# Which engine's queue holds the empty instruction between the two chains of an output product

## The chip, the cores and the metric

The program runs on one core of a Trainium2 chip, as one launch. The metric is the device time of that launch in microseconds (us). Before the change three runs took 1582.14, 1582.5 and 1580.37 us; their median is 1582.14 us. One more execution was profiled; it took 1579.73 us, and its trace spans 1577.9 us. All times inside the program are counted from the start of that span.

Five engines run their own queues of instructions in order and meet only at semaphores: TensorE (PE in the rows, PEld for its weight loads), VectorE (DVE), ScalarE (ACT), GpSimd (POOL) and SyncE (SP). SyncE computes nothing here; its queue issues nearly all transfers. A q behind an engine's name in a row (SPq, ACTq) marks what its sequencer does by itself: issuing a transfer, or waiting.

## The reference

Two attentions over 2048 rows with 32 heads of 18 columns (D = 576), each with its own input and weights; the outputs stand side by side. The first (A) looks at 8 keys per row, at distances 0, 2, ... 14; the second (B) at all 2048 keys.

```python
def _A_ref(x, wqkv, wo):          # W, dil = 8, 2
    qkv = (x @ wqkv) -> q, k, v
    idx = pos[:, None] - arange(W)[None, :] * dil
    logits = einsum("bhsd,bhswd->bhsw", q, k[idx]) * scale   # masked where idx < 0
    o = einsum("bhsw,bhswd->bhsd", softmax(logits), v[idx])
    return o.reshape(B, S, D) @ wo
def _B_ref(x, wqkv, wo):
    qkv = (x @ wqkv) -> q, k, v
    p = softmax(einsum("bhqd,bhkd->bhqk", q, k) * scale)
    o = einsum("bhqk,bhkd->bhqd", p, v)
    return o.reshape(B, S, D) @ wo
return concatenate([_A_ref(A...), _B_ref(B...)], axis=-1)
```

## The kernel before

After the projections (until about 470 us) the program walks through 512 steps. A step is one group of four heads, one block of 512 queries and one tile of 128 keys: `NG` = 8 groups of 64 steps, a block every 16. In a step TensorE makes four banks of scores (line 285), ScalarE takes their exponentials (line 293), TensorE multiplies these with the values and adds up in the bank `po` (line 766). Beside that TensorE makes scores once more for a block that comes later (line 161), of which VectorE takes the maxima (line 169).

The order of each engine's queue is that in which the Python code calls its instructions; nothing rearranges it. Work with a due time is put on an agenda by step (`later`, `plan`) and called by `due` when its step comes. So the transfers that SyncE issues stand in one line, in the order of the steps, and a transfer that waits for something holds up all behind it.

Which transfers stand there in this phase:

- after a block of queries: the denominators are taken out of the result (`den<-o`, line 809), their reciprocals are written to memory (`drec<-den`, line 811) and read back spread over the rows (`rec<-drec`, line 812), some steps later the finished block is stored (`do<-n`, line 801). Line 812 waits until the write of line 811 has landed;
- the rows of a coming group's queries and keys (`qs<-dqk`, line 144, and `ks<-dqk`, line 143), 288 KB each;
- the row maxima put into a coming block (`qs<-mh` and `qs<-mt`, line 200), 2 KB each;
- for attention A, which runs on GpSimd: its inputs (`aq<-da`, `akv<-da`, line 974) and results (`dao<-...`, line 1044), and the results read back as operands of its output product (`at<-dao`, `ahl<-dao`, lines 1059 and 1061).

An output product of A is 28 small matmuls (line 1347) in two chains: one on the lower half of TensorE's rows, one on the upper half, both adding into one bank of PSUM. `together` lays such a product over two steps. It calls the first chain among the scores and maxima of the odd heads, then an empty instruction, then the second chain among those of the even heads. The empty instruction (line 1358) waits for the last matmul of the first chain (line 1359), and the first matmul of the second chain waits for the empty instruction (line 1362), so that no matmul of the second chain starts into the bank before the first chain is done. There are 32 such pairs of steps, at 610 us to 1460 us; 27 of them stand ahead of the last group. TensorE's queue goes on in order: while the first matmul of the second chain waits, no score, maximum or product behind it starts.

ScalarE's queue at that place holds the exponentials of the pair; the one that stands behind the empty instruction belongs to a score that TensorE makes ahead of the second chain.

Of the kernel before, what the change touches and what calls it, by code (L numbers as in the profile page):

```python
# [22 lines left out]
NG = H // 4  # L23
# [38 lines left out]
def two_attentions(ctx: ExitStack, tc, xa, wa, woa, xb, wb, wob, out):  # L62
# [5 lines left out]
    nc = tc.nc  # L68
# [13 lines left out]
    def bank(kind=None):  # L82
        r = rings[kind or ring]
        r.append(r.pop(0))
        return p_bank.tile([128, 512], F32, name=f"bank{r[-1]}")
# [154 lines left out]
    def maximum(r, ps=None):  # L240

        ps = ps or bank()
        (take, reduce), piece = next_piece(r)
        take(ps, *piece)
        return lambda: reduce(ps, *piece)
# [4 lines left out]
    def sync(ins, other):  # L250

        tc.add_manual_dep(ins.ins, other.ins.name,
                          mybir.DependencyInfo(mybir.DependencyClass.Sync, mybir.DependencyReason.DATA), reason="one bank")
# [24 lines left out]
    def score(g, b, kt, h, kind="scores", between=None, put_off=False):  # L278

        assert (g, b) in placed  # L280
        qs, ks = sets[g % 3]
        p, r = divmod(h, 2)
        ps = bank(kind)
        at = slice(64 * r, 64 * r + 56)
        awaiting(nc.tensor.matmul(ps, ks[at, p, 128 * kt : 128 * kt + 128], qs[at, b, p], start=True, stop=True))  # L285
        if between:
            between()

        def exponential():
            counted[0] += 1  # L290
            early = counted[0] % 12 < 6
            e = (e_room if early else work).tile([128, 512], F32, name="e", bufs=6)
            nc.scalar.activation(e, ps, AF.Exp, scale=SCALE)  # L293
            return e

        return exponential if put_off else exponential()
# [1032 lines left out]
    def together(both, y):  # L1329

        at = [(*divmod(s // NT, NB), s % NT) for s in (step, step + 1)]
        es = [[None] * 4 for _ in range(2)]
        ps = bank("scores")[:, : y.shape[1]]
        held = rings["scores"].pop()
        exps = deque()

        def one(i, h):
            f = score(*at[i], h, put_off=True)
            exps.append(lambda: es[i].__setitem__(h, f()))

        def others(r):
            return [f for i in range(2) for h in (r, r + 2)
                    for f in (lambda i=i, h=h: one(i, h), lambda: maximum(r)())[:: 1 - 2 * r]]

        def piece(r, k):
            a, b = both[r][k]
            return nc.tensor.matmul(ps, a, b, start=r == k == 0, stop=r == 1 and k == len(both[1]) - 1)  # L1347

        def in_turn(*lanes):

            for _, f in sorted(((at + every * k, f) for fs, at, every in lanes for k, f in enumerate(fs)), key=lambda p: p[0]):
                f()
                while len(exps) > 1:
                    exps.popleft()()

        last = []
        in_turn(([lambda k=k: last.append(piece(0, k)) for k in range(len(both[0]))], 0, 133), (others(1), 1, 235))
        between = nc.scalar.nop()
        sync(between, last[-1])
        upper = others(0)  # L1360
        if leaving:
            upper[2] = lambda f=upper[2], copy=leaving.pop(): (f(), exps.popleft()(), copy())
        in_turn(([lambda k=k: sync(piece(1, k), between) if k == 0 else piece(1, k) for k in range(len(both[1]))], 240, 133),
                (upper, 0, 235))
        while exps:
            exps.popleft()()
        nc.scalar.activation(y, ps, AF.Copy)
        rings["scores"].append(held)
        rings["scores"].append(rings["scores"].pop(0))
        return [(*at[i], es[i]) for i in range(2)]  # L1370
# [4 lines left out]
    while step < ALL:  # L1375
# [6 lines left out]
        if inside and inside[0] in for_two and kt and len(ready) == 1 and total - sum(given) >= 8 and step + 4 < ALL:  # L1382
            new = together(*inside.pop(0)(False))
            assert not leaving
            due()
            step += 1
            weigh(*ready, new[0])
            ready[:] = new[1:]
            due()
            step += 1  # L1390
            continue
# [77 lines left out]
```

## Time and profile before

| what | before |
|---|---|
| median of three runs | 1582.14 us |
| profiled execution, its own time | 1579.73 us |
| span of its trace | 1577.9 us |
| TensorE busy | 1569.6 us (99%), granted clock 1.0 |
| VectorE busy | 1377.1 us (87%) |
| ScalarE busy | 1207.4 us (77%) |
| GpSimd busy | 969.7 us (61%) |
| transfers issued by SyncE | 1036 |
| empty instructions on line 1358 | 32, all in ScalarE's queue |

A busy share is an average over phases with different limits, and the end of a matmul is modelled, so that 99% doesn't mean that TensorE works at its peak. Idle time of an engine that isn't the one waited for costs nothing. A row of the timeline gives the start in us, the length in us, the engine, the source line and what is written from what; a number behind an x says how many instructions are merged in it. For an instruction that only waits, and for a transfer's issue, the row begins when the wait is over: the wait is the empty time ahead of it. The length of an issue is the time on SyncE; when the data has landed shows only in who waits for it. A row of the view of stretches gives the stretch, its length, the busy time of each engine, then the granted clock, the mean busy share of the 16 transfer engines and GB/s.

### The profile page before, as it was taken

What the parts mean: (1) busy time and instruction counts of PE and PEld (TensorE: products, weight loads), DVE (VectorE), ACT (ScalarE), POOL (GpSimd) and SP (SyncE); (2) the same over time, 40 slices, a digit from 0 to 9 for tenths busy, and PEclk for the clock granted to TensorE, in tenths of its full rate; (3) what the DMA queues carried; (4) which work ended last, traced back from release to release, by engine and by line L of the source; (5) the groups of instructions that cost most, each with busy time, mean ns of one, the idle gap of its engine ahead of it and who ended that gap; (6) DMA issues with size and microseconds to landing.
All of it is one profiled execution on the core that took longest, in us unless ns stands there. A gap on an engine that the chain in (4) does not pass through costs nothing.

```text
span 1577.9 us, 34942 instructions
## 1 busy us (share of the span) xinstructions
PE 1569.6 (99%) x13272; PEld 966.4 (61%) x13272; DVE 1377.1 (87%) x2333; ACT 1207.4 (77%) x2411; POOL 969.7 (61%) x803
## 2 busy tenths in 40 slices
PE   9999999999999999999999999999999999999998
PEld 7998899999644445445445445444444444545686
DVE  5289999999999999999989999999999999998633
ACT  6424432121799999999999999999999999998654
POOL 2416742210266995995896897897798799682000
PEclk9999999999999999999999999999999999999999
DMA  9948954532312362245325325421721332154311
GB/s 242 240 147 218 270 164 131 138 107 81 62 41 65 73 142 77 64 122 108 75 77 131 89 81 117 120 79 50 149 85 50 91 95 57 51 167 131 140 57 69
DMA packets 188168, 175.65 MB, mean 111 GB/s; under 512 B 119432, under 2 KB 133512, under 8 KB 186272
## 3 DMA queue, kind: packets, MB, share of 16 engines
q1 hardware_dynamic: 182992, 161.73, 37.4%
q0 software_dynamic: 4032, 10.63, 3.3%
q8 instruction: 104, 1.70, 0.5%
q10 hardware_dynamic: 976, 1.07, 0.2%
q14 instruction: 64, 0.52, 0.1%
HBM read 98.77 MB, written 73.47 MB: 109 GB/s over the span
## 4 chain that ended last, share of the span: by engine, by line
PE 93%; DVE 3%; DMA 3%; ACT 1%; SPq 0%; issue 0%; DVEq 0%; ACTq 0%
PE po L766 30%; PE bank L285 19%; PE bank L161 17%; PE bank L380 14%; PE bank L1347 4%; PE bank L1244 3%; PE bank L571 2%; DVE mx L169 2%; PE bank L317 2%; DMA dqk<-ohi 1%; DMA dqk<-olo 1%; DMA qs<-mh 0%; PE bank L1212 0%; ACT e L293 0%; DMA raw<-xa 0%; SPq L530 0%
## 5 line engine op out<-in xcount | busy, mean ns | idle before, releaser
L169 DVE TENSOR_REDUCE mx<-bank 128x2 f32<-128x512 f32 x2048 | 1278.1, 684 | 109.1 <-PE bank L161 81.9
L293 ACT ACTIVATE e<-bank 128x512 f32<-128x512 f32 x2048 | 1047.9, 605 | 80.5 <-PE bank L285 78.0
L161 PE MATMUL bank<-ks,qs 54*128 54x512 f32 (+1 forms) x2464 | 785.8, 380 | 1.6 <-ACT y L1249 0.3
L161 PEld LDWEIGHTS bank<-ks,qs 54*128 54x128 f32 x2464 | 403.2, 184 | 387.6 <-DVE mx L169 341.1
L285 PE MATMUL bank<-qs,ks 56*128 56x512 f32 x2048 | 592.8, 426 | 0.1
L766 PE MATMUL po<-e,v 128*19 128x512 f32 x4096 | 531.7, 599 | 0.5
L285 PEld LDWEIGHTS bank<-qs,ks 56*128 56x128 f32 x2048 | 309.1, 185 | 21.3 <-ACT e L293 14.6
L987 POOL TENSOR_TENSOR pr<-aq,akv 128x1024 f32<-128x1024 f32 x72 | 158.3, 2200 | 16.7 <-PE po L766 13.8
L1029 POOL TENSOR_TENSOR pr<-lg,akv 128x1024 f32<-128x1024 f32 x72 | 158.3, 2198 | 0.6
L766 PEld LDWEIGHTS po<-e,v 128*19 128x19 f32 x4096 | 73.7, 97 | 138.2 <-issue 132.9
L991 POOL TENSOR_TENSOR pr<-pr 128x1024 f32<-128x1024 f32 x64 | 152.6, 2384 | 5.0
L715 ACT ACTIVATE ohi<-bank 128x512 f32<-128x512 f32 (+1 forms) x56 | 30.4, 594 | 149.2 <-issue 134.3
L380 PE MATMUL bank<-xhi,ahi 64*128 64x512 f32 (+1 forms) x448 | 112.9, 386 | 0.0
L380 PE MATMUL bank<-xhi,alo 64*128 64x512 f32 (+1 forms) x448 | 111.7, 387 | 0.0
L380 PE MATMUL bank<-xlo,ahi 64*128 64x512 f32 (+1 forms) x448 | 110.4, 387 | 0.0
L1347 PE MATMUL bank<-wohi,at 64*128 64x288 f32 x480 | 103.3, 305 | 0.0
L1030 POOL TENSOR_TENSOR pr<-pr 128x512 f32<-128x512 f32 x72 | 92.4, 1284 | 5.6
L430 POOL TENSOR_TENSOR alo<-raw,ahi 128x512 fp32r<-128x512 f32 (+1 forms) x14 | 17.6, 1254 | 122.6 <-ACT ahi L429 94.6
L1347 PEld LDWEIGHTS bank<-wohi,at 64*128 64x128 f32 x480 | 74.6, 184 | 27.6 <-ACT e L293 23.8
L525 POOL TENSOR_TENSOR olo<-olo,ohi 128x512 fp32r<-128x512 f32 x36 | 46.2, 1293 | 70.3 <-ACT ohi L524 60.6
L104 POOL CAST mh<-mt 128x32 fp32r<-128x32 f32 x32 | 6.7, 210 | 114.0 <-DVE mt L186 114.0
L1347 PE MATMUL bank<-wolo,at 64*128 64x288 f32 x240 | 70.3, 293 | 0.0
(210 smaller groups left out, 1864.9 us busy)
## 6 DMA issues: line engine op xcount, KB each, us to landing
do<-n SPq DMA_DIRECT2D x30, 512.0 KB
da<-ohi SPq DMA_DIRECT2D x52, 256.0 KB
akv<-da SPq DMA_DIRECT2D x64, 175.5 KB
out<-y SPq DMA_DIRECT2D x31, 288.0 KB
qs<-dqk SPq DMA_DIRECT2D x30, 288.0 KB
ks<-dqk SPq DMA_DIRECT2D x30, 288.0 KB
at<-dao SPq DMA_DIRECT2D x60, 128.0 KB
rec<-drec SPq DMA_DIRECT2D x29, 256.0 KB
```

The costliest lines, as they stand in the source:

```text
L161: return awaiting(nc.tensor.matmul(ps if part is None else ps[:, 256 * r : 256 * r + 256], qs[at, b, p, 128 * t : 128 * t + 128], ks[at, p ...
L169: nc.vector.tensor_reduce(at, ps.rearrange("q (s n) -> q s n", s=2), axis=AX.X, op=ALU.max)
L285: awaiting(nc.tensor.matmul(ps, ks[at, p, 128 * kt : 128 * kt + 128], qs[at, b, p], start=True, stop=True))
L293: nc.scalar.activation(e, ps, AF.Exp, scale=SCALE)
L380: nc.tensor.matmul(ps, a, b, start=start, stop=stop)
L766: nc.tensor.matmul(po[32 * i : 32 * i + 19], vs[g][:, kt, 19 * i : 19 * i + 19], es[i], start=kt == 0, stop=kt == NT - 1)
L987: nc.gpsimd.tensor_mul(pr, ap(st["q"][:, 2 * c], (SUB, 2), (0, W), (1, SUB)), window(st["k"], c))
L991: nc.gpsimd.tensor_add(st["pr"], st["pr"], pr)
L1029: nc.gpsimd.tensor_mul(at, ap(st["lg"], (0, 2), (SUB, W), (1, SUB)), window(st["v"], c))
L1030: nc.gpsimd.tensor_add(at[:, :, :4], at[:, :, :4], at[:, :, 4:])
L1244: nc.tensor.matmul(sums_[r], *both[r][i], start=i == 0, stop=last)
L1347: return nc.tensor.matmul(ps, a, b, start=r == k == 0, stop=r == 1 and k == len(both[1]) - 1)
```

## The change

The empty instruction goes into SyncE's queue, except where the first of the two steps is in the last group.

```diff
         last = []
         in_turn(([lambda k=k: last.append(piece(0, k)) for k in range(len(both[0]))], 0, 133), (others(1), 1, 235))
-        between = nc.scalar.nop()
+        between = (nc.scalar if at[0][0] == NG - 1 else nc.sync).nop()
         sync(between, last[-1])
```

27 of the 32 move, 5 stay. No matmul, exponential, maximum or transfer is added, removed or called in another order; the empty instruction itself has no row below, its waits show at the next row of its queue and at the matmul that waits for it.

TensorE's queue, at the first matmul of the second chain (line 1347) of the pair at 715 us; - is before, + is the change:

```order
 L285 MATMUL bank_11203<-qs_3497,ks_3498 128x512 [waits Activation_49]
 L161 MATMUL bank_11207<-ks_89,qs_88 128x512 [waits DVE_49]
-L1347 MATMUL bank_11161<-wohi,at_10878 128x288 [waits Activation_sequencer_49]
+L1347 MATMUL bank_11161<-wohi,at_10878 128x288 [waits SP_sequencer_49]
 L1347 MATMUL bank_11161<-wohi,at_10879 128x288
 L285 MATMUL bank_11212<-qs_3497,ks_3498 128x512 [waits Activation_49]
```

The matmul stands where it stood; it now waits for SyncE's sequencer. The rows behind it, scores (line 285) and the rest of the chain, are held with it.

SyncE's queue at the same pair; akv are inputs of attention A, DMAHW are the semaphores of earlier transfers:

```order
 L812 DMA rec<-drec 128x1x512 [waits DMAHW4_49,DMAHW1_49]
 L974 DMA akv<-da 32x18x78 [waits DMAHW5_49]
-L974 DMA akv<-da 32x18x78 [waits DMAHW6_49]
+L974 DMA akv<-da 32x18x78 [waits PE_49,DMAHW6_49]
 L809 DMA den<-o 128x1x16 [waits DMAHW7_49,Activation_49]
 L302 DMA v<-dv 128x1216 [waits DMAHW0_49]
```

The empty instruction stands ahead of the second `akv<-da`: behind `rec<-drec`, which waits for two transfers, and ahead of `den<-o`.

SyncE's queue at the pair at 961 us:

```order
 L812 DMA rec<-drec 128x1x512 [waits DMAHW7_49,DMAHW5_49]
 L974 DMA akv<-da 32x18x78 [waits DMAHW0_49]
-L144 DMA qs_88<-dqk 18x8x512 [waits DMAHW1_49,PE_49]
+L144 DMA qs_88<-dqk 18x8x512 [waits PE_49,DMAHW1_49]
 L200 DMA qs_1511<-mh 2x8x32 [waits DMAHW2_49,Pool_49]
 L200 DMA qs_1511<-mh 2x8x32 [waits DMAHW3_49]
```

Here the empty instruction stands ahead of a load of query rows and of the row maxima; the wait for TensorE that now comes first in the row of line 144 is that of the empty instruction.

## The prediction

> **What bounds the kernel now.** First the page's busy times and its chain of waits.
>
> ```profile
> PE 1569.6 (99%) x13272; PEld 966.4 (61%) x13272; DVE 1377.1 (87%) x2333; ACT 1207.4 (77%) x2411; POOL 969.7 (61%) x803
> PE 93%; DVE 3%; DMA 3%; ACT 1%; SPq 0%; issue 0%; DVEq 0%; ACTq 0%
> ```
>
> The chain that ends last runs on TensorE for 93% of the span and on SyncE's queue for none of it. So a microsecond in which TensorE's queue stands still lengthens the program by nearly as much, while SyncE may wait as it likes as long as nobody waits for SyncE. The change makes TensorE wait for SyncE at 27 places.
>
> Next, what one such place costs today: the view of line 1358, all of it and at the pair at 715 us, and TensorE's timeline there.
>
> ```profile
> L1358 ACTq EVENT_SEMAPHORE  x32: 17/17/17, 610.1 to 1460.4; - x32
> L1358 ACTq EVENT_SEMAPHORE  x1: 17/17/17, 715.8 to 715.8; - x1
> 715.36 0.29 PE L1347 MATMUL bank<-wolo,ahl 64*128 64x288 f32 x1
> 715.80 0.41 PE L161 MATMUL bank<-ks,qs 54*128 54x512 f32 x1
> 715.83 0.40 PE L1347 MATMUL bank<-wohi,at 64*128 64x288 f32 x1
> ```
>
> The first chain ends at 715.36 + 0.29 = 715.65, the empty instruction runs at 715.8, the second chain starts at 715.83. Both signals together take 0.18 us, and the matmul of line 161 that stands ahead of it in the queue starts only at 715.80. So the wait is hidden but for 0.03 us. The last thing to read is therefore SyncE's timeline: is SyncE past the row ahead of the empty instruction when the first chain ends?
>
> **What is removed.** If SyncE answered at once, the second chain could start with the matmul ahead of it: at most 0.03 us earlier here, some 27 x 0.03 = 0.8 us in all. How fast SyncE answers TensorE can be read where a load of operands waits for the last matmul of a product.
>
> ```profile
> 624.16 0.29 PE L1347 MATMUL bank<-wohi,ahl 64*128 64x288 f32 x1
> 624.47 0.36 SPq L1059 DMA_DIRECT2D at<-dao  x1
> 607.35 2.15 SPq L200 DMA_DIRECT2D qs<-mt  x4
> ```
>
> 624.47 - 624.45 = 0.02 us: no slower than ScalarE's sequencer. I take nothing for an open place, with -0.8 us as one end, and +0.05 us for each of the 27, or +1.4 us, as the other (a signal that took half of today's 0.18 us path more). The last row shows the tightest of the open places: the transfers ahead of the first empty instruction are issued by 607.35 + 2.15 = 609.50, and the first row of line 1358 is at 610.1. At 24 of the 27 places SyncE's timeline has the row ahead issued before the empty instruction's present time, so that it would be standing ready.
>
> The 17 ns of the empty instruction's row say nothing of this. [...] By the rows alone the change would cost 27 x 0.017 = 0.5 us.
>
> **The three places where SyncE is late.** At the pair at 715 us SyncE's timeline and its longest wait read:
>
> ```profile
> 709.89 0.35 SPq L811 DMA_DIRECT2D drec<-den  x1
> 712.20 0.59 SPq L974 DMA_DIRECT2D akv<-da  x1
> 724.18 0.60 SPq L812 DMA_DIRECT2D rec<-drec  x1
> 724.83 0.55 SPq L974 DMA_DIRECT2D akv<-da  x1
> SPq L812 <- DMA drec<-den: 8.1, 1, 8.1
> ```
>
> The empty instruction will stand behind the transfer at 724.83. That one is issued by 725.38, because `rec<-drec` ahead of it waits for the write of the reciprocals (`drec<-den`), which was issued at 709.89 and has landed only at 724.18. Nothing in this wait depends on TensorE. With 0.1 us for the signals (the rest of the 0.18 us once TensorE has long signalled) the second chain starts at 725.48 instead of 715.83: **9.6 us**. All of TensorE's queue stands behind it, so it is lost whole. The same at 854 us and at 1136 us:
>
> ```profile
> 854.74 0.40 PE L1347 MATMUL bank<-wohi,at 64*128 64x288 f32 x1
> 849.45 0.35 SPq L811 DMA_DIRECT2D drec<-den  x1
> 862.14 0.57 SPq L812 DMA_DIRECT2D rec<-drec  x1
> 862.81 0.59 SPq L809 DMA_DIRECT2D den<-o  x1
> ```
>
> Here the empty instruction stands between line 812 and line 809: free at 862.71, start at 862.81 instead of 854.74, **8.1 us**.
>
> ```profile
> 1136.14 0.40 PE L1347 MATMUL bank<-wohi,at 64*128 64x288 f32 x1
> 1126.49 0.35 SPq L811 DMA_DIRECT2D drec<-den  x1
> 1137.63 0.59 SPq L812 DMA_DIRECT2D rec<-drec  x1
> 1138.27 0.56 SPq L974 DMA_DIRECT2D akv<-da  x1
> ```
>
> Free at 1138.83, start at 1138.93 instead of 1136.14: **2.8 us**. Together 20.5 us.
>
> Why the small write takes 14.3, 12.7 and 11.1 us there shows against a calm place:
>
> ```profile
> 633.01 0.33 SPq L811 DMA_DIRECT2D drec<-den  x1
> 634.98 0.59 SPq L812 DMA_DIRECT2D rec<-drec  x1
> 1105.00:1136.00 31.00, 31.00 (x255) 14.19 (x254) 29.62 (x52) 29.90 (x60) 22.51 (x22) 1.00 0.76 158
> ```
>
> With nothing ahead of it, it is answered in 2.0 us; at the late places 288 KB loads of rows stand ahead of it in the same queue, and the transfer engines are busy for 0.76 of the stretch.
>
> [...]
>
> **What is held back.** At places where SyncE now runs ahead, the rows behind the empty instruction wait for TensorE from now on. Mostly that is a load needed much later. It matters where held rows pile up in front of a later late write. At 1103 us:
>
> ```profile
> 1103.67 0.40 PE L1347 MATMUL bank<-wohi,at 64*128 64x288 f32 x1
> 1101.08 2.40 SPq L144 DMA_DIRECT2D qs<-dqk  x3
> 1103.53 0.61 SPq L974 DMA_DIRECT2D aq<-da  x1
> 1104.18 1.55 SPq L144 DMA_DIRECT2D qs<-dqk  x2
> ```
>
> Five loads of rows move back by up to 1103.6 - 1101.1 = 2.5 us, and from 1105 to 1136 the transfer engines have no pause (the row above), so the write at 1126.49 lands later by 0 to 2.5 us; nearer to the upper end, I take 2. At 961 us:
>
> ```profile
> L1358 ACTq EVENT_SEMAPHORE  x1: 17/17/17, 960.8 to 960.8; - x1
> 955.24 0.82 SPq L144 DMA_DIRECT2D qs<-dqk  x1
> 956.16 2.29 SPq L200 DMA_DIRECT2D qs<-mh  x4
> 958.55 2.56 SPq L200 DMA_DIRECT2D qs<-mt  x4
> 963.15 4.00 SPq L144 DMA_DIRECT2D qs<-dqk  x5
> 965.00:995.00 30.00, 29.95 (x250) 14.21 (x246) 29.08 (x53) 28.65 (x57) 13.00 (x9) 1.00 0.64 148
> 994.40 0.58 SPq L812 DMA_DIRECT2D rec<-drec  x1
> 995.55 0.60 SPq L974 DMA_DIRECT2D aq<-da  x1
> 997.50 0.39 PE L1347 MATMUL bank<-wohi,at 64*128 64x288 f32 x1
> ```
>
> The load and eight small transfers, issued from 955.24 to 961.11 (5.9 us), start at 960.8 at the earliest and end at 966.7; with line 809 (0.59 us at 862.81 above, 0.7 to the next row) the loads of 963.15 begin at 967.4, 4.3 us later. The transfer engines are busy without pause to 995 (0.64). If the whole 4.3 us reach the write ahead of `rec<-drec` at 994.40, the row ahead of the next empty instruction is issued not by 996.15 but by 1000.45, and the second chain of the pair at 997.50 starts 3.0 us late. Bounds 0 and 3.0; I take 2, since part may be made up on the way. One load each is held ahead of the other two late places:
>
> ```profile
> 675.73 0.84 SPq L144 DMA_DIRECT2D qs<-dqk  x1
> ```
>
> This one would wait for the pair at 681 us, some 5.5 us; the row behind it (`den<-o`) waits for ScalarE until after that pair, as now, so nothing more is held. The load itself takes the transfer engines a part of these microseconds later on: 0 to 1 us, I take 0.5 for both places.
>
> **What is given back.** While TensorE stands, VectorE and ScalarE work off what they hold. In the row of 965 to 995 they are busy 29.08 and 28.65 of 30 us, so they hold little; 0 to 3 us over three stalls, I take 1.
>
> **Sum**, in us: 9.6 + 8.1 + 2.8 + 2 + 2 + 0.5 - 1 = 24. Against the profiled execution's own time: 1579.73 + 24 = 1603.7. The median of the runs is 2.4 us above that execution, so I forecast 1582.1 + 24 = **1606 us**.
>
> **The rivals.**
> *More places become late.* For it: held rows shift the whole queue, and open places have little room (0.6 us at 610 us). Against it: most held rows are followed by a row that waits for TensorE or ScalarE anyway. Three more stalls like the smallest, 3 x 2.8, on top of the upper bounds of the held terms (2.5 + 3 + 1): 20.5 + 6.5 + 8.4 = 35 us, 1617 us.
> *Half of the stalls vanish.* The write lands earlier once TensorE's later rows push no transfers, or other engines make good more than I allow. Against it: the loads ahead of the write are issued before the stall. 10 us, 1592 us.
> *SyncE is in time everywhere.* Only if the write were answered in the 2.0 us of the calm place. Then just the open places count: no change, 1582 us.
> *Faster.* ScalarE's queue no longer stands at the empty instruction until the first chain ends; if the exponential behind it is what TensorE waits for next, each of the 27 pairs gains up to the 0.18 us of today's path: 27 x 0.18 = 4.9 us, 1577 us. It decides only if the three late places are in time as well. Against it: the second chain starts 0.03 us behind the matmul ahead of it.
>
> **How the numbers follow.** Chances: forecast 0.66 (its own range 1600 to 1612), more late places 0.14, half of the stalls 0.12, in time everywhere 0.04, faster 0.04. About 0.2% (3 us) is what a measurement of this kernel can tell from no change. The range of 8 in 10 reaches from between the halved case and the forecast to near the case of more late places: 1596 to 1616. Slower: 0.66 + 0.14 + 0.12 = 0.92; same 0.04; faster 0.04.
>
> **What would show it.** Right: the row of line 1358 on SyncE 27 times; TensorE with a hole of about 9.6, 8 and 3 to 5 us at the pairs that are now at 715, 854 and 1136 us, each ended by SyncE right behind `rec<-drec`, and one of 1 to 3 us at the pair now at 997; the chain of waits with some 2% on line 811's write; other pairs as long as now. Wrong: no such holes, holes at many more pairs, or a second chain that starts later than now at open places.

## The result and the profile after

The changed kernel takes 1615.87 us (median of four runs, 1614.43 to 1617.46) against 1582.02 us of the kernel before on the same chip: a ratio of 1.022, 95% interval 1.0209 to 1.0232, or 33.9 us more. The forecast was 24 us more. The profiled execution took 1614.43 us, its trace spans 1612.6 us, 34.7 us more than before; the following is told by that trace.

First the page of the changed kernel: busy times, the clock in 40 slices (a digit is tenths of full speed, 9 is 90% or more), the chain of waits.

```profile
PE 1579.4 (98%) x13272; PEld 972.4 (60%) x13272; DVE 1378.3 (85%) x2333; ACT 1207.0 (75%) x2411; POOL 970.4 (60%) x803
PEclk9999999999999999999998999999999999999999
PE 79%; DMA 7%; DVE 2%; SPq 1%; ACT 0%; issue 0%; POOL 0%; DVEq 0%; ACTq 0%
```

With the same 13272 matmuls TensorE is busy 1579.4 us, 9.8 us longer than before; the mean granted clock of the run is 0.99 instead of 1.0, and one slice shows an 8. Transfers now make 7% of the chain, where they made 3%.

Line 1358, and what waits for it (in the second part: idle time in us, how often, longest):

```profile
L1358 SPq EVENT_SEMAPHORE  x27: 17/17/17, 609.7 to 1399.1; - x27
L1358 ACTq EVENT_SEMAPHORE  x5: 17/17/17, 1417.3 to 1495.2; - x5
```

```profile
PE bank L1347 <- SPq L1358: 24.4, 4, 8.2
```

27 empty instructions are SyncE's, as the diff says, and TensorE waits for SyncE at exactly four places. Its timeline there (idle time ahead of a row in brackets), and the second chain of the pair behind the first hole:

```profile
723.71 0.60 PE L1347 MATMUL bank<-wohi,at 64*128 64x288 f32 x1 [7.75 <-SPq L1358]
873.75 0.61 PE L1347 MATMUL bank<-wohi,at 64*128 64x288 f32 x1 [8.16 <-SPq L1358]
1022.03 0.40 PE L1347 MATMUL bank<-wohi,at 64*128 64x288 f32 x1 [2.71 <-SPq L1358]
1168.38 0.60 PE L1347 MATMUL bank<-wohi,at 64*128 64x288 f32 x1 [5.77 <-SPq L1358]
...
755.07 0.40 PE L1347 MATMUL bank<-wohi,at 64*128 64x288 f32 x1
```

The same row of the kernel before:

```profile
744.50 0.40 PE L1347 MATMUL bank<-wohi,at 64*128 64x288 f32 x1
```

The four are the pairs that stood at 715, 854, 997 and 1136 us. Taking each pair's start in the old trace from that in the new gives the loss step by step: the 715 pair starts 723.71 - 715.83 = 7.9 us later, but the next pair 755.07 - 744.50 = 10.6 us later. So 2.7 us are lost between the two pairs, where no empty instruction stands. It is the same behind each hole:

| pair, time before | forecast | lost at the hole, counted from the pair before | lost from there to the next pair |
|---|---|---|---|
| 715 us | 9.6 | 8.1 | 2.7 |
| 854 us | 8.1 | 8.75 | 2.8 |
| 997 us | 2 | 3.1 | 1.6 |
| 1136 us | 2.8 + 2 | 6.4 | 2.2 |
| two held loads | 0.5 | in the rows above | |
| everywhere else | -1 (given back) | -0.9 | |
| sum | 24 | 25.4 | 9.3 |

25.4 + 9.3 = 34.7 us, the difference of the spans. Where SyncE stands at the late places (its timeline):

```profile
709.32 0.35 SPq L811 DMA_DIRECT2D drec<-den  x1
722.40 0.60 SPq L812 DMA_DIRECT2D rec<-drec  x1
723.05 1.23 SPq L974 DMA_DIRECT2D akv<-da  x2
860.16 0.35 SPq L811 DMA_DIRECT2D drec<-den  x1
873.06 0.58 SPq L812 DMA_DIRECT2D rec<-drec  x1
1021.34 0.59 SPq L974 DMA_DIRECT2D aq<-da  x1
1155.11 0.35 SPq L811 DMA_DIRECT2D drec<-den  x1
1167.07 0.59 SPq L812 DMA_DIRECT2D rec<-drec  x1
1167.71 0.56 SPq L974 DMA_DIRECT2D akv<-da  x1
```

Each hole ends within 0.11 us of the row ahead of the empty instruction: 723.05 + half of 1.23 is 723.67 and the matmul starts at 723.71; 873.64 and 873.75; 1021.93 and 1022.03; 1168.27 and 1168.38. At the third, `rec<-drec` is issued at 1020.20 and two more rows stand between it and the empty instruction. At the three late places of the prediction `rec<-drec` follows its write by 13.1, 12.9 and 12.0 us (14.3, 12.7 and 11.1 before).

What is lost behind the holes shows in the view of stretches (after the five busy times: granted clock, share of the transfer engines, GB/s):

```profile
715.40:719.30 3.90, 0.56 (x4) 0.13 (x2) 1.53 (x3) 1.74 (x4) 3.82 (x2) 1.00 0.62 157
719.30:723.70 4.40, 0.00 (x0) 0.00 (x0) 0.00 (x0) 0.00 (x0) 4.24 (x3) 0.51 0.57 117
723.70:729.50 5.80, 5.79 (x31) 3.65 (x35) 2.08 (x3) 2.20 (x4) 4.30 (x3) 0.50 0.90 151
729.50:735.00 5.50, 5.50 (x48) 2.44 (x40) 4.14 (x9) 4.30 (x9) 2.00 (x3) 0.99 0.48 79
...
873.70:879.70 6.00, 5.95 (x31) 3.65 (x35) 2.94 (x7) 2.20 (x4) 0.47 (x2) 0.50 0.13 45
1023.00:1026.40 3.40, 3.40 (x24) 1.77 (x24) 1.89 (x3) 1.75 (x4) 2.05 (x3) 0.52 0.70 152
1168.40:1173.30 4.90, 4.90 (x27) 3.44 (x31) 2.08 (x3) 2.20 (x4) 2.45 (x3) 0.50 0.83 145
```

TensorE's idle time in the first hole begins at 723.71 - 7.75 = 715.96; 3.3 us later, at 719.3, the granted clock falls to a half. It is still at a half when TensorE starts again, for another 5.8 us, and then back at once. The 31 matmuls of that stretch have a spacing of 5.8 / 31 = 0.19 us, the 48 of the next 5.5 / 48 = 0.11 us. The four stretches at half clock with TensorE at work add up to 5.8 + 6.0 + 3.4 + 4.9 = 20.1 us; done at half speed, that would lose 10 us, and 9.3 us are missing. The output product itself shows the pace, two matmuls of the first chain ahead of the hole and two of the second behind it:

```profile
714.87 0.29 PE L1347 MATMUL bank<-wolo,at 64*128 64x288 f32 x1
715.01 0.29 PE L1347 MATMUL bank<-wohi,ahl 64*128 64x288 f32 x1
...
724.12 0.44 PE L1347 MATMUL bank<-wohi,at 64*128 64x288 f32 x1
724.36 0.44 PE L1347 MATMUL bank<-wolo,at 64*128 64x288 f32 x1
```

One follows the other after 0.14 us ahead of the hole and 0.24 us behind it.

So at the first hole the clock is at a half (0.50) from 719.3 to 729.5, 10.2 us, and behind the third for 3.4 us. How long TensorE has to stand for it, these four places don't tell: the third hole idles for 2.71 us only, and the clock falls all the same.

### The profile page after: what moved, and what is told of

The parts are those of the page before. It is cut to its first block, busy times and chain, and to the rows that moved or that the text cites. A ratio compares the mean times of both kernels' runs of the same rounds, so it can differ in the third digit from the quotient of the medians.

```text
span 1612.6 us, 34942 instructions
## 1 busy us (share of the span) xinstructions
PE 1579.4 (98%) x13272; PEld 972.4 (60%) x13272; DVE 1378.3 (85%) x2333; ACT 1207.0 (75%) x2411; POOL 970.4 (60%) x803
## 4 chain that ended last, share of the span: by engine, by line
PE 79%; DMA 7%; DVE 2%; SPq 1%; ACT 0%; issue 0%; POOL 0%; DVEq 0%; ACTq 0%
PE po L766 28%; PE bank L285 17%; PE bank L161 15%; PE bank L380 11%; PE bank L1347 4%; PE bank L1244 3%; DMA drec<-den 3%; DVE mx L169 2%; DMA qs<-dqk 1%; DMA do<-n 1%; DMA dqk<-olo 1%; DMA dqk<-ohi 0%; PE bank L1212 0%; DMA at<-dao 0%; PE bank L1176 0%
## 5 line engine op out<-in xcount | busy, mean ns | idle before, releaser
L1347 PE MATMUL bank<-wohi,at 64*128 64x288 f32 x480 | 107.1, 313 | 24.4 <-SPq L1358 24.4
L380 PE MATMUL bank<-xlo,ahi 64*128 64x512 f32 (+1 forms) x448 | 114.5, 387 | 0.0
```

What stands on the lines that cost most here:

```text
L380: nc.tensor.matmul(ps, a, b, start=start, stop=stop)
```

## The experiments

The diffs stand against the changed kernel and leave out the lines that count. `turn_of` in them counts the calls of `together` from 0, so that 4, 8, 14 and 18 are the four pairs with a hole. Each time stands beside the median of the kernel before on the same chip (1580.29 to 1580.56 us). The theory is: the loss is four holes and the half clock behind them, and nothing else.

**The open places alone.** The 23 other empty instructions stand on SyncE.

```diff
-        between = (nc.scalar if at[0][0] == NG - 1 else nc.sync).nop()
+        between = (nc.scalar if at[0][0] == NG - 1 or turn_of[0] in (4, 8, 14, 18) else nc.sync).nop()
```

> The empty instruction goes to SyncE at 23 of the 27 pairs; the pairs that had a hole (now at 715, 865, 1019 and 1162 us of the changed kernel) keep it on ScalarE. Theory (only the holes and TensorE's halved clock behind them cost time): no hole, granted clock 1.0 throughout, time of the kernel before, 1582 us within 2 us. Rival (each signal through SyncE, or the holding back of transfers, costs something too): 1585 us or more, with second chains that start later at the 23 pairs.

1582.28 us, ratio 1.0013 (1.0004 to 1.0022): 2 us of the 34, no wait of TensorE for SyncE, clock 1.0. So an open place costs nothing that counts. The 2 us come up behind the 17th and the 28th pair: there TensorE waits 1.1 us for VectorE's maxima (line 169) and 0.7 us for row maxima that a transfer puts into a block (`qs<-mt`, line 200), where it waited for neither before. Why these come later is not settled.

**Transfers held, without a wait of TensorE.** The kernel before, with a second empty instruction on SyncE that waits for the first chain but that nobody waits for.

```diff
-        between = (nc.scalar if at[0][0] == NG - 1 else nc.sync).nop()
+        between = nc.scalar.nop()
         sync(between, last[-1])
+        if at[0][0] < NG - 1:
+            sync(nc.sync.nop(), last[-1])
```

> The kernel before, with its empty instructions on ScalarE, and at the 27 pairs a second one in SyncE's queue that waits for the end of the first chain and that nobody waits for: SyncE's transfers are held back as in the change, TensorE waits for ScalarE alone. Theory (holding back transfers matters only by making SyncE later where TensorE waits for it): no holes, granted clock 1.0, the kernel before within 3 us. Rival (transfers that come late stop TensorE or GpSimd by themselves): 5 us or more above it.

1582.28 us, ratio 1.0007 (0.9998 to 1.0016). Holding transfers back costs 2.5 us at most, the end of the interval, as long as TensorE doesn't wait for what stands behind them.

**Three late places alone.**

```diff
-        between = (nc.scalar if at[0][0] == NG - 1 else nc.sync).nop()
+        between = (nc.sync if turn_of[0] in (4, 8, 18) else nc.scalar).nop()
```

> The empty instruction goes to SyncE at three pairs alone, those where the trace of before had SyncE late (715, 854, 1136 us); so nothing is held back ahead of them. Theory (holes as read from the trace of before, plus half of the time that TensorE runs at half clock behind each): holes of 9.6, 8.1 and 2.8 us, behind the two long ones some 2.7 us each, behind the short one 0 to 1.7 us: 20.5 + 5.4 to 7.1, so 1608 to 1610 us; the pair at 997 us has no hole. Rival (the extra time of the change came from holding back alone): 1582 + 20.5 = 1602.5 us.

1603.49 us, ratio 1.0143 (1.0126 to 1.016): 23.2 us more, between the two expectations. By its trace the holes take 9.1, 9.0 and 2.0 us, 20.1 in all, and the stretches behind them 2.1, 2.3 and 0.2 us. Both parts are there behind the two long holes. The third, without holders ahead of it, shrinks from 6.4 to 2.0 us, and behind it the clock stays full (its row of the timeline, and the stretch behind it):

```profile
1159.40 0.40 PE L1351 MATMUL bank<-wohi,at 64*128 64x288 f32 x1 [1.66 <-SPq L1362]
1159.20:1162.50 3.30, 3.10 (x31) 2.12 (x35) 1.89 (x3) 1.92 (x4) 3.14 (x4) 1.00 0.61 121
```

The 997 pair has no hole, but it tells nothing here, since its empty instruction stays on ScalarE in this kernel.

**TensorE kept busy in the holes.** The change, and ahead of the second chain at the four late pairs 56, 58, 16 and 40 matmuls into a free bank whose result nobody uses: added work, about as long as each hole.

```diff
+        whi = wo["a"][0][0]
+        def first_of_upper():
+            n = {4: 56, 8: 58, 14: 16, 18: 40}.get(turn_of[0], 0)
+            room = bank() if n else None
+            for _ in range(n):
+                nc.tensor.matmul(room[:, :288], whi[:, :128], whi[:, :288], start=True, stop=True)
+            sync(piece(1, 0), between)
-        in_turn(([lambda k=k: sync(piece(1, k), between) if k == 0 else piece(1, k) for k in range(len(both[1]))], 240, 133),
+        in_turn(([first_of_upper if k == 0 else lambda k=k: piece(1, k) for k in range(len(both[1]))], 240, 133),
```

> The change, and at the four pairs with holes 56, 58, 16 and 40 extra matmuls of 128x288 into a spare bank right ahead of the second chain (their result is not used); at 0.132 us each, as the 280 of line 317 take, they fill 7.4, 7.7, 2.1 and 5.3 us of the holes of 8.1, 8.6, 3.1 and 6.2 us. Theory (TensorE's clock is halved because it stood idle): the holes end when they did, the granted clock stays at 1.0, and the time falls by the 9.2 us that come behind the holes: some 1607 us. Rival (what comes behind the holes is the refilling of ScalarE's and VectorE's queues): 1615 us or more, as the change.

1608.03 us, ratio 1.0174 (1.0159 to 1.019): by the ratios (1.022 - 1.0174) x 1580 = 7.3 us faster than the change, with 170 matmuls more. TensorE's timeline and two stretches of this kernel at the first late pair:

```profile
716.14 7.65 PE L1373 MATMUL bank<-wohi 128*128 128x288 f32 x56
723.84 0.40 PE L1351 MATMUL bank<-wohi,at 64*128 64x288 f32 x1
```

```profile
715.40:724.00 8.60, 8.55 (x65) 7.90 (x63) 1.79 (x3) 1.98 (x5) 8.36 (x4) 1.00 0.56 138
724.00:730.00 6.00, 6.00 (x55) 3.20 (x56) 3.65 (x6) 3.79 (x8) 4.57 (x4) 1.00 0.86 151
```

The second chain starts at 723.84, as late as in the change, since SyncE is as late as there; but the clock stays at 1.00 and the next 6 us hold 55 matmuls. From each of the four holes to the next pair nothing is lost now (-0.03, -0.01, -0.02 and 0.0 us), where the change lost 9.3 us. This settles the second part. The rival, that the time behind a hole goes to filling ScalarE's and VectorE's queues again, would have stayed: they stood still just as long.

**The read back two steps later.**

```diff
-        times = (1, 10, 11, 14, 20, 21, 22, 26) if g < NG - 1 else (1, 6, 7, 10, 13, 14, 15, 16)
+        times = (1, 10, 11, 16, 20, 21, 22, 26) if g < NG - 1 else (1, 6, 7, 10, 13, 14, 15, 16)
```

> The change, and the read back of the reciprocals (line 812) is due two steps later in all groups but the last, so that it stands behind the empty instruction in SyncE's queue at the pairs with holes. Theory (SyncE is late there only because this one row waits ahead of the empty instruction): no hole over 1 us, granted clock 1.0, 1582 to 1585 us. Rival (the loads in front make any row late at these places, or the row makes another pair late): holes stay, 1595 us or more.

1615.39 us, ratio 1.0215 (1.0199 to 1.0231): as the change. It missed its aim. Two steps move `rec<-drec` behind one more pair of inputs, but not behind the empty instruction; the holes stay at 8.8, 9.6, 2.3 and 5.4 us. It tells nothing between the theories.

**The read back four steps later,** 18 in place of 14 in the same line; now it stands behind the empty instruction.

> The change, and the read back of the reciprocals (line 812) due four steps later, so that it stands behind the empty instruction at all four pairs with holes. Theory (this one wait ahead of the empty instruction makes the holes): what is left ahead of the empty instruction is issued at most some 1.5 us after the end of the first chain, so holes of 0 to 1.5 us, granted clock 1.0, the kernel before and 0 to 5 us. Rival (any row at these places is late because of the loads in front of it): holes of 5 us and more stay, 1600 us or more.

1608.3 us (1603.5 to 1615.53, a wider spread than any other), ratio 1.0175 (1.0146 to 1.0204). The holes shrink from 8.1, 8.75, 3.1 and 6.4 to 3.7, 2.0, none and 3.5 us. So with the wait of `rec<-drec` about half of the first and the last hole goes, most of the second and all of the third; the rest are rows ahead of the empty instruction that are late too. The time lies where the rival put it (1600 us and more), the holes lie between the two expectations. SyncE's timeline and its and TensorE's waits in this kernel:

```profile
716.01 6.95 SPq L974 DMA_DIRECT2D akv<-da  x3
```

```profile
SPq L974 <- DMA ks<-dqk: 6.0, 3, 3.1
```

```profile
PE bank L1347 <- DMA at<-dao: 2.9, 2, 2.1
```

Inputs of attention A wait for loads of keys. The time doesn't fall by as much as the holes: the clock still halves behind three of them (3.4 to 6.8 us), a first chain now waits for its operands (`at<-dao`), and 5.3 us are lost ahead of the 29th pair: there TensorE waits 2.4 us for row maxima (`qs<-mt`), and the clock is at a half for 6.8 us, from 1434.3 on.

**The last hole, with and without holders.** In one kernel the pairs at 961, 997, 1103 and 1136 us are on SyncE, in the other those at 997 and 1136 us alone. (The expectation names the pair at 961 us by its time in the changed kernel, 982 us.)

```diff
-        between = (nc.scalar if at[0][0] == NG - 1 else nc.sync).nop()
+        between = (nc.sync if turn_of[0] in (12, 14, 17, 18) else nc.scalar).nop()
```

```diff
-        between = (nc.scalar if at[0][0] == NG - 1 else nc.sync).nop()
+        between = (nc.sync if turn_of[0] in (14, 18) else nc.scalar).nop()
```

> The empty instruction goes to SyncE at the pairs now at 1005-30 and 1019 us and at 1129 and 1162 us of the changed kernel (the 13th, 15th, 18th and 19th): the pair with a hole and the pair ahead that holds back loads. Theory (the loads held back by the pair ahead land later and make the write late): holes as in the change, 3.1 us and 6.1 us, and behind them 1.6 and 2.2 us at half clock: 13 us above the kernel before. Rival (the holes come from being later in the program after the first two): the holes that the trace of before shows, 0 and 2.8 us, so 3 to 5 us above it.

> The same without the pairs ahead: the empty instruction goes to SyncE at the 15th and 19th pair alone. Theory: no hole at the 15th, 2 to 2.8 us at the 19th, granted clock 1.0 or halved for one short piece: 2 to 4 us above the kernel before. Rival (holding back has no part in it): the holes of the change, 3.1 and 6.1 us, 13 us above it.

With holders 1593.48 us, ratio 1.0072 (1.0057 to 1.0087), 12.9 us more; without 1583.94 us, ratio 1.0023 (1.0012 to 1.0033), 3.4 us more. The hole at the 997 pair is 3.1 us with and absent without, that at the 1136 pair 6.2 and 2.3 us. SyncE's and TensorE's timelines with holders, then without:

```profile
1108.42 2.40 SPq L144 DMA_DIRECT2D qs<-dqk  x3
1114.30 4.89 SPq L143 DMA_DIRECT2D ks<-dqk  x1
1134.48 0.35 SPq L811 DMA_DIRECT2D drec<-den  x1
1145.70 0.59 SPq L812 DMA_DIRECT2D rec<-drec  x1
1147.00 0.60 PE L1351 MATMUL bank<-wohi,at 64*128 64x288 f32 x1 [5.83 <-SPq L1362]
```

```profile
1099.97 2.41 SPq L144 DMA_DIRECT2D qs<-dqk  x3
1106.52 3.40 SPq L143 DMA_DIRECT2D ks<-dqk  x1
1124.68 0.36 SPq L811 DMA_DIRECT2D drec<-den  x1
1136.01 0.59 SPq L812 DMA_DIRECT2D rec<-drec  x1
1137.31 0.40 PE L1351 MATMUL bank<-wohi,at 64*128 64x288 f32 x1 [1.92 <-SPq L1362]
```

At the pair at 1103 us the one kernel is 5.8 us behind the other (second chain at 1108.35 and 1102.57). The held loads go out 8.45 us later, 2.7 beyond that; the load of keys behind them takes SyncE 1.5 us longer to issue (4.89 against 3.40); the write of line 811 goes out 9.80 us later, 4.0 beyond. From the write to the read back it is 11.2 and 11.3 us. So what is held comes back whole, and grows: the write isn't answered later, it is issued later.

**The write and the read back on ScalarE's queue,** in the change and in the kernel before. (A ring, in the expectations, is the line of transfers that one engine issues.)

```diff
-                                 lambda: load(drec[g, b].rearrange("i (p n) -> (i p) n", n=16), den),
-                                 lambda: load(rec, rows(drec[g, b], (512, 4), (0, 32), (1, 512))),
+                                 lambda: (load if g == NG - 1 else nc.scalar.dma_start)(drec[g, b].rearrange("i (p n) -> (i p) n", n=16), den),
+                                 lambda: (load if g == NG - 1 else nc.scalar.dma_start)(rec, rows(drec[g, b], (512, 4), (0, 32), (1, 512))),
```

> The change, and the write and the read back of the reciprocals (lines 811 and 812) are issued by ScalarE in all groups but the last, so that they stand in its ring and not behind the loads in SyncE's. Theory (the write is late because it stands behind 288 KB loads in the same ring): it is answered in 2 to 4 us; SyncE's empty instruction is held only by rows that wait for an earlier transfer, so holes of 0 to 3.7 us at the four pairs; 0 to 10 us above the same edit of the kernel before. Rival (the 16 transfer engines are busy, whatever the ring): the write takes 8 us and more there too, ScalarE stands behind it, and the time is 15 us or more above the kernel before.

> The same edit of lines 811 and 812 in the kernel before, with all empty instructions on ScalarE: what the edit itself costs. Theory: some 28 times 1 us of issue on ScalarE, of which what is not hidden shows, 0 to 15 us above the kernel before; no hole at any empty instruction. Rival (the write is slow in ScalarE's ring too): ScalarE stands up to 8 us and more at the pairs that are late, 15 us or more above the kernel before.

1641.99 us, ratio 1.0383 (1.0366 to 1.0401), and 1616.86 us, ratio 1.0222 (1.0206 to 1.0237). With the edit in both, the change is 25 us slower than the kernel before, where 0 to 10 us were expected; the edit alone costs the kernel before 36 us, where 0 to 15 us were expected. A miss as a test. The place of 715 us in the kernel before with this edit, and a wait of TensorE there:

```profile
713.70 0.33 ACTq L811 DMA_DIRECT2D drec<-den  x1
719.90 0.54 ACTq L812 DMA_DIRECT2D rec<-drec  x1
```

```profile
PE bank L1347 <- DMA at<-dao: 9.8, 3, 6.7
```

The read back follows its write by 6.2 us where it was 14.3 us, which is the distance of the steps at which the two are called: here the write is answered in time. That does not tell the order of the queue from the load of the transfer engines. In the 1.5 us behind the write these are busy for 0.05 here and for 0.95 in the kernel before (stretches of this kernel, then of the kernel before):

```profile
713.70:715.20 1.50, 1.50 (x14) 0.61 (x8) 1.36 (x4) 1.50 (x4) 1.42 (x2) 1.00 0.05 6
709.90:711.40 1.50, 1.50 (x15) 0.47 (x11) 1.37 (x4) 1.50 (x4) 1.42 (x2) 1.00 0.95 204
```

And at 565 us in the same kernel, where the transfer engines are busy for 0.77 of the 5 us behind the write, the read back follows by 8.4 us (565.09 and 573.52). So a write can be late without loads ahead of it in its own queue.

The cost of the edit shows in other waits. In the kernel before with this edit TensorE waits 9.8 us for operands of first chains, 8.9 us for another empty instruction in ScalarE's queue (line 265, 4.0 us at the longest) and 5.7 us for a load of keys, and the mean granted clock is 0.99. SyncE's rows wait for earlier transfers (the DMAHW of the rows). In the changed kernel with this edit its waits between 862 and 892 us show that some of these are now issued by ScalarE: a row of maxima that has nothing to do with the denominators waits 7.9 us for their read back. TensorE waits for SyncE's empty instruction at three pairs there, 12.7 us in all, 8.2 us at the longest. SyncE's wait:

```profile
SPq L200 <- DMA rec<-drec: 7.9, 1, 7.9
```

So the price of a queue for these two alone was not measured. No kernel of the study is faster than the one before.

## Why the prediction was right in kind and short in size

**What bounds it, and the open places: right.** Time that TensorE stands is lost whole (24.4 us of waits at the four pairs, 26.4 us lost there); 23 moved instructions alone cost 2 us of 34. (By its own reason, half of 0.18 us more at each place, the upper end for 27 places is 2.4 us, not the 1.4 us of the prediction.) TensorE waits for SyncE at the four pairs that the prediction named and at no other. The two rivals without a loss expected no such wait, and the one of more late places expected more of them. That the time lies nearer to the 1617 us of that rival than to 1606 us is chance: no further place was late.

**The late write: right, sizes off by little.** The holes at 715 and 854 us measured 8.1 and 8.75 us, with their held loads included, against 9.6 + 8.1 + 0.5. At 715 us the write was answered 1.2 us sooner than in the trace before. By itself the 1136 place gives 2.0 to 2.3 us in two experiments (2.8 forecast). The reason that the prediction gives for the late write, loads ahead of it in the same queue, is not shown: busy transfer engines would fit as well, and at 565 us a write was late in a queue of its own.

**What is held back: the mechanism right, the bound too low.** At 1136 us the hole with holders is 6.2 to 6.4 us, 4 us longer than without, where the prediction put 2 and at most 2.5. Its step "the write at 1126.49 lands later by 0 to 2.5 us" took the hold as a delay of the landing and bounded it by the move of the held rows. It is a delay of the issue, and the rows behind the held ones add 1.5 us to it. At 997 us 3.1 us against 2, at the upper bound of 3.0. Nothing was made up on the way.

**What is given back: not shown.** The sum has 0.9 us of it against 1, but 0.4 us of these are there at the first pair (607.45 against 607.88 us), ahead of every hole; that is the difference of two executions.

**The step that failed.** "All of TensorE's queue stands behind it, so it is lost whole": the sum priced a stall at its own length, and its only term for what follows was a gain. What follows is a loss. The clock halves inside the hole, or 1.1 us behind it at the third, and stays so for 3.4 to 6 us of work: 2.7, 2.8, 1.6 and 2.2 us, together 9.3 us, almost all of the 10 us by which the forecast fell short. With TensorE kept busy in the holes the 9.3 us were gone. The view that would have told it, the granted clock, was in rows that the prediction quoted, at 1.00 throughout: the longest wait of TensorE in the kernel before is 1.5 us, its clock is 1.0, and the prediction took that as given.

**What stays open:** why the two waits behind the 2 us of the open places come up, and how much of the 11 to 14 us of the late write is the queue's order and how much the load of the transfer engines, since the experiment on ScalarE's queue took both away at these places and changed other waits as well.

## What to carry to other kernels

Before an instruction on which the bounding engine waits goes into another engine's queue, read what stands ahead of it there: SyncE's queue, 0% of the chain of waits before, kept TensorE waiting for 2.71 to 8.16 us at the four places where one of its transfers waited for an earlier one to land. Price a stall of TensorE by its length and by the clock behind it: here 1.6 us for a hole of 3 us, 2.7 us for one of 8; behind 1.60 us of idle time it halved in one kernel, behind 1.66 us it stayed full in another. Where the wait cannot be moved, matmuls that nobody uses can fill it: here they kept the clock at 1.00 and gave back 7.3 us.

## What the runs showed of the hardware

- In the trace of the change, from the first hole to behind the last, the granted clock is at a half from 719.35 to 729.59, 869.53 to 879.77, 1023.13 to 1026.55 and 1166.49 to 1173.32 us, 10.2, 10.2, 3.4 and 6.8 us long, and at 1.00 between them. It fell 3.4, 3.9 and 3.9 us after the idle time of the first, second and fourth hole began, and 1.1 us after the third hole had ended. It was full again after TensorE had worked at a half for 5.9, 6.0, 3.4 and 4.9 us.
- The length of a hole alone did not tell whether the clock fell. With the read back four steps later, TensorE is idle for 3.30 - 1.70 = 1.60 us of the stretch from 860.90, and the next stretch is at 0.50; without holders it stands 1.92 us, and the clock is 0.50 from 1138 on; in the kernel with three late places it stands 1.66 us, and the clock stays at 1.00 (stretch from 1159.20). What decides was not shown. The stretches show the kernel with the read back four steps later, then the one without holders (hole of 2.3 us).

```profile
860.90:864.20 3.30, 1.70 (x19) 1.70 (x19) 1.78 (x5) 2.24 (x6) 0.00 (x0) 1.00 0.64 138
864.30:867.60 3.30, 3.30 (x18) 0.51 (x16) 1.82 (x5) 0.72 (x2) 0.46 (x2) 0.50 0.58 137
...
1138.00:1139.00 1.00, 1.00 (x10) 1.00 (x9) 0.69 (x1) 0.83 (x2) 0.90 (x2) 0.50 0.37 105
```

- Where the transfers held by the last holder went out, the issue of a 288 KB load took SyncE 4.89 us in place of 3.40; a load of the same line 20 us later is issued in 0.55 us. The row shows no wait for a semaphore in that time; what held the issue was not tried.
